# A Hedgehog attention and gMLP kernel: three-stage pipeline over batches, wide exponentials, token layout s = 4p + c

## The chip, the cores and the metric

The kernel runs on one core of a Trainium2 chip. The metric is device time in microseconds, as the median of several executions: 618.6 us before the change (runs of 616.49, 618.60 and 618.83 us).

## What is computed

Two layers run one after the other. The first is a linear attention for 8 batches, 8 heads, 576 tokens and 64 values per head:

```
phi(x):  proj = x @ w_phi                       # 64 -> 128
         proj = proj - max(|proj|)              # per token
         return [exp(proj), exp(-proj)]         # 256 features
kv  = phi(k)^T v          z = sum over tokens of phi(k)
out = (phi(q) kv) / (phi(q) z + 1e-6)
```

The heads side by side give x of 576 x 512 for each batch. The second layer, with 512 -> 1024 features, is

```
h = relu(x @ w_in);  u, v = halves of h
v_n = (v - mean(v)) / sqrt(var(v) + 1e-6)
v_s = w_spatial @ v_n + b_spatial               # over the 576 tokens
out = (u * v_s) @ w_out
```

All matmul operands are bf16 and PSUM sums are fp32. Before the change the kernel takes the exponentials of q without their row maximum; after it the maximum is subtracted. Both leave out the 1e-6 in the quotient's denominator.

## The kernel before

Work comes in 32 tasks, one for a batch and a pair of heads. A batch's 576 tokens are cut into four blocks of 128 and one of 64.

`load_batch` (L101) brings in q, k and v with 15 transfers, all issued by GpSimd, each 64 numbers (256 bytes) per token and head. `stageA` transposes q and k of two heads (L125, L131), copies them out of PSUM on ScalarE and VectorE (L128, L134) and, for each token block, makes k's projection (L139), its row maxima (L143, L147) and four exponentials of 128 columns whose bias is the row's maximum (L150, L152). q's projection is made transposed, so its features stand in partitions, in pieces of 512 and 64 tokens (L159), with two exponentials each (L162, L164). `stageB` sums k's features against v with a column of ones (L181), copies the result (L185), multiplies by q's features (L192), divides (L197, L199), transposes (L205) and copies into `xT_b` (L208).

`stage2` runs once per batch, after the batch's last pair: v's half of the first product with relu, mean, variance, a square root on ScalarE, reciprocal and normalization (L219 to L237), u's half (L247, L251), the spatial product (L259, L263), and the output product, copied out by VectorE and stored by SyncE (L269 to L275). The bias row of the spatial product stands as row 64 of the fifth token block.

The loop is software-pipelined by one task: `stageA` of task i, then `stageB` of task i-1, and `stage2` after every fourth. A scheduler puts each engine's instructions in a fixed order when the program is built. PSUM's eight banks are split into two for transposes, two shared by k's projection and the quotients, one for k's sums and three for everything else. All weights, w_spatial with its 25 transposes among them, are loaded ahead of the first batch.

## Time and profile before

| what | value |
|---|---|
| median of 3 runs | 618.6 us (616.49 to 618.83) |
| profiled execution: span from its first to its last instruction | 615.2 us |
| profiled execution: time outside the span | not recorded apart; the runs lie 1.3 to 3.6 us above the span |
| TensorE matmuls, busy | 448.6 us, 73% |
| ScalarE, busy | 380.9 us, 62% |
| VectorE, busy | 335.8 us, 55% |
| GpSimd, busy | 111.2 us, 18% |
| mean granted TensorE clock | 0.721 |

Busy time is the union of an engine's instructions. The share is an average over the whole span, so it says nothing of which engine ends which stage. The granted clock is a share of 2.4 GHz; it takes the two values 1.0 (2.4 GHz) and 0.5 (1.2 GHz), and a value between is a stretch with some of each. Matmuls overlap in the engine's pipeline, and the end of each is modelled, so a duration of one is longer than the distance from one start to the next.

### The profile page before, as it was taken

What the parts mean: (1) busy time and instruction counts of PE and PEld (TensorE: products, weight loads), DVE (VectorE), ACT (ScalarE), POOL (GpSimd) and SP (SyncE); (2) the same over time, 40 slices, a digit from 0 to 9 for tenths busy, and PEclk for the clock granted to TensorE, in tenths of its full rate; (3) what the DMA queues carried; (4) which work ended last, traced back from release to release, by engine and by line L of the source; (5) the groups of instructions that cost most, each with busy time, mean ns of one, the idle gap of its engine ahead of it and who ended that gap; (6) DMA issues with size and microseconds to landing.
All of it is one profiled execution on the core that took longest, in us unless ns stands there. A gap on an engine that the chain in (4) does not pass through costs nothing.

```text
span 615.2 us, 8892 instructions
## 1 busy us (share of the span) xinstructions
PE 448.6 (73%) x2969; PEld 219.4 (36%) x2969; DVE 335.8 (55%) x1243; ACT 380.9 (62%) x1116; POOL 111.2 (18%) x144
## 2 busy tenths in 40 slices
...
GB/s 126 125 113 18 58 58 2 18 60 78 38 2 69 21 70 34 1 78 55 62 0 1 78 77 39 1 69 22 70 35 0 78 2 1 0 29 50 1 2 77
DMA packets 119966, 26.47 MB, mean 43 GB/s; under 512 B 113712, under 2 KB 114800, under 8 KB 119920
## 3 DMA queue, kind: packets, MB, share of 16 engines
...
## 4 chain that ended last, share of the span: by engine, by line
PE 47%; ACT 36%; DVE 7%; DMA 5%; issue 3%; POOL 1%; DVEq 0%; ACTq 0%; POOLq 0%
ACT k_feat L152 8%; ACT k_feat L150 7%; PE ps_kv L181 7%; PE ps_v L219 6%; PE ps_s L259 6%; PE ps_num L192 5%; ACT q_featT L162 5%; PE ps_u L247 5%; PE ps_o L269 5%; ACT q_featT L164 4%; PE ps_k L131 4%; DMA w_sp_tmp<-in_moe_w_spatial_dram 3%; ACT qT L128 3%; PE ps_qp L159 3%; ACT L231 3%
## 5 line engine op out<-in xcount | busy, mean ns | idle before, releaser
L150 ACT ACTIVATE k_feat<-ps_kp,negm 128x128 bf16<-128x128 f32 (+1 forms) x320 | 121.9, 381 | 23.7 <-DVE negm L143 23.4
L152 ACT ACTIVATE k_feat<-ps_kp,m 128x128 bf16<-128x128 f32 (+1 forms) x320 | 122.5, 383 | 8.2 <-DVE negm L143 4.1
L143 DVE TENSOR_REDUCE negm<-ps_kp 128x2 f32<-128x256 f32 (+1 forms) x160 | 67.4, 423 | 80.9 <-PE ps_kp L139 67.4
L162 ACT ACTIVATE q_featT<-ps_qp 128x512 bf16<-128x512 f32 (+1 forms) x128 | 53.7, 424 | 91.4 <-PE ps_qp L159 91.4
L139 PE MATMUL ps_kp<-wphi,kT 128*128 128x256 bf16 (+1 forms) x160 | 57.8, 364 | 52.3 <-ACT k_feat L152 44.3
L181 PE MATMUL ps_kv<-v_aug,k_feat 128*128 128x65 bf16 (+1 forms) x640 | 81.6, 229 | 15.0 <-ACT k_feat L150 14.8
L110 POOL DMA_DIRECT2D q_bf<-in_q_dram x40 | 34.8, 873 | 278.6 <-PE ps_q L125 277.2
L181 PEld LDWEIGHTS <-k_feat 128*128 128x128 bf16 (+1 forms) x640 | 48.1, 111 | 98.0 <-ACT k_feat L150 80.8
L199 DVE TENSOR_SCALAR attn_pair<-ps_num,recip 128x64 bf16<-128x64 f32 (+1 forms) x320 | 71.4, 273 | 1.1
L247 PE MATMUL ps_u<-xT_b,w_in_bf 128*128 128x512 bf16 (+1 forms) x256 | 55.7, 371 | 18.0 <-ACT uT L251 14.3
L219 PE MATMUL ps_v<-w_in_bf,xT_b 128*128 128x512 bf16 (+1 forms) x160 | 68.0, 573 | 1.1 <-DVE xT_b L208 0.9
L128 ACT COPY qT<-ps_q 128x576 bf16<-128x576 bf16 x32 | 20.7, 646 | 76.3 <-PE ps_q L125 61.0
L192 PE MATMUL ps_num<-kv_sb,q_featT 128*128 128x65 bf16 (+1 forms) x640 | 55.2, 233 | 12.5 <-ACT k_feat L152 9.4
L197 DVE RECIPROCAL recip<-ps_num 128x2 f32<-128x2 f32 (+1 forms) x160 | 26.6, 169 | 59.3 <-PE ps_num L192 57.4
L164 ACT ACTIVATE q_featT<-ps_qp 128x512 bf16<-128x512 f32 (+1 forms) x128 | 53.4, 421 | 0.0
L192 PEld LDWEIGHTS <-q_featT 128*128 128x128 bf16 (+1 forms) x640 | 41.4, 125 | 29.0 <-issue 23.7
L247 PEld LDWEIGHTS <-w_in_bf 128*128 128x128 bf16 x256 | 23.4, 117 | 61.7 <-issue 56.7
L205 PE MATMUL ps_a<-ident,attn_pair 128*128 128x128 bf16 (+1 forms) x160 | 43.1, 270 | 1.1 <-DVE attn_pair L199 0.9
L159 PE MATMUL ps_qp<-qT,wphi_two 64*128 64x64 bf16 (+1 forms) x128 | 32.9, 384 | 15.1 <-ACT q_featT L164 13.4
L114 POOL DMA_DIRECT2D v_aug<-in_v_dram x40 | 34.1, 872 | 47.5 <-PE ps_qp L159 47.4
L259 PE MATMUL ps_s<-w_spatT,v_n 128*128 128x512 bf16 (+2 forms) x320 | 40.9, 285 | 0.0
L147 DVE TENSOR_SCALAR m<-negm 128x2 f32<-128x2 f32 (+1 forms) x160 | 33.4, 209 | 12.4 <-DVE negm L143 0.5
...
## 6 DMA issues: line engine op xcount, KB each, us to landing
...
q_bf<-in_q_dram POOLq DMA_DIRECT2D x32, 128.0 KB, 4.5
k_bf<-in_k_dram POOLq DMA_DIRECT2D x32, 128.0 KB, 4.6
v_aug<-in_v_dram POOLq DMA_DIRECT2D x32, 128.0 KB, 4.8
...
out_dram<-out_sb SPq DMA_DIRECT2D x8, 128.0 KB, 2.3
...
w_out_bf<-in_moe_w_out_dram POOLq DMA_DIRECT2D x4, 128.0 KB, 6.7
```

The costliest lines, as they stand in the source:

```text
L139: nc.tensor.matmul(out=ps_kp[:sl, :], lhsT=kT[:, s0:s0 + sl], rhs=wphi2, start=True, stop=True)
L143: nc.vector.tensor_reduce(out=negm2[:sl, :], in_=ps_kp[:sl, :].rearrange("p (h f) -> p h f", h=2), axis=AX.X, op=ALU.max, apply_absolute_v ...
L150: nc.scalar.activation(out=k_feat[:sl, ci, hh, 0:F], in_=ps_kp[:sl, hh * F:(hh + 1) * F], func=AF.Exp, bias=negm2[:sl, hh:hh + 1], scale=1.0)
L152: nc.scalar.activation(out=k_feat[:sl, ci, hh, F:2 * F], in_=ps_kp[:sl, hh * F:(hh + 1) * F], func=AF.Exp, bias=m2[:sl, hh:hh + 1], scale= ...
L162: nc.scalar.activation(out=q_featT[:, hh, 0, t0:t0 + tw], in_=ps_qp[:F, :tw], func=AF.Exp, bias=0.0, scale=1.0)
L164: nc.scalar.activation(out=q_featT[:, hh, 1, t0:t0 + tw], in_=ps_qp[:F, :tw], func=AF.Exp, bias=0.0, scale=-1.0)
L181: nc.tensor.matmul(out=ps_kv[:, hh, fc, :], lhsT=k_feat[:sl, ci, hh, fc * F:(fc + 1) * F], rhs=v_aug[:sl, ci, h, :], start=(ci == 0), stop ...
L192: nc.tensor.matmul(out=ps_num[:sl, hh, :], lhsT=q_featT[:, hh, fc, s0:s0 + sl], rhs=kv_sb[:, hh, fc, :], start=(fc == 0), stop=(fc == 1))
L199: nc.vector.tensor_scalar(out=attn_pair[:sl, ci, hh * D:(hh + 1) * D], in0=ps_num[:sl, hh, 0:D], scalar1=recip2[:sl, hh, :], scalar2=None, ...
L219: nc.tensor.matmul(out=ps_v[:sl, :], lhsT=xT_b[:, kc, s0:s0 + sl], rhs=w_in_bf[:, kc, HALF:DFF], start=(kc == 0), stop=(kc == KC - 1))
L247: nc.tensor.matmul(out=ps_u[:, :tw], lhsT=w_in_bf[:, kc, dc * P:(dc + 1) * P], rhs=xT_b[:, kc, t0:t0 + tw], start=(kc == 0), stop=(kc == K ...
L259: nc.tensor.matmul(out=ps_s[:, :tw], lhsT=v_n[:kl, sc, dc * P:(dc + 1) * P], rhs=w_spatT[:kl, sc, t0:t0 + tw], start=(sc == 0), stop=(sc = ...
```

## The change

The kernel's body is written anew around the same arithmetic.

* **Layout.** Token s = 4p + c stands in partition p, so that one transfer brings four tokens (1 KB) per partition and head, and a batch has four full blocks of 128 rows. The 64 tokens beyond 512 of two batches stand together in one tile of 128 rows (the "tail").
* **k.** The exponentials are taken over 512 columns (four blocks of a head) without a bias. The row maxima go into v instead: GpSimd multiplies v by exp(-m) for the first half of the features and by exp(m) for the second (`scale_v`). v is loaded in fp32 by SyncE.
* **q.** The row maxima are found on a second, untransposed projection, brought into bf16 high and low parts by GpSimd, transposed, and subtracted in PSUM by a third matmul against a selection matrix (`main_m`, `a2_unit`).
* **Quotient.** One reciprocal and one multiplication for four heads.
* **Second layer.** It runs for two batches at once, on nine blocks of 128 tokens. The reciprocal square root is a power of -0.5 on GpSimd, for four blocks at a time. ScalarE copies the outputs. `u` is multiplied in place.
* **Order.** Step n does the first stage of batch n, the second (q's features, k's sums) of batch n-1 and the third (quotients) of batch n-2, with the second layer of an earlier batch pair merged in between from step 4 on. The last pair's second layer stands alone at the end. The first batch's k and q are loaded ahead of the weights, and w_spatial is transposed in step 1.
* **PSUM.** One bank for all transposes, three for projections, two for sums and quotients, two for the second layer.

The core of the diff:

```diff
+    def load(b):
+        d = dict(
+            q=ld.tile([P, H, NB * D], BF16, tag="q_bf", name="q_bf"),
...
+        nc.gpsimd.dma_start(out=d["k"], in_=main_ap(k, b))
+        nc.gpsimd.dma_start(out=d["q"], in_=main_ap(q, b))
+        nc.sync.dma_start(out=d["v"].rearrange("p (h c) d -> p h (c d)", h=H), in_=main_ap(v, b))
...
+    def a1_unit(b, pj):
...
+        kT = a1.tile([P, 2, 2, P], BF16, tag="kT")
+        nc.scalar.copy(out=kT, in_=pt[:, 0])
+        nc.scalar.copy(out=d["qT"][:, pj].rearrange("p h (c t) -> p h c t", c=2), in_=pt[:, 1])
         for hh in range(2):
             h = 2 * pj + hh
+            pk = ps_pj.tile([P, NB, F], FP32, tag="pj")
+            for cp in range(2):
+                nc.tensor.matmul(out=pk[:, 2 * cp:2 * cp + 2, :], lhsT=kT[:, hh, cp, :], rhs=wphi2,
+                                 start=True, stop=True)
+            kf = feat.tile([P, 2, NB, F], BF16, tag="kf", bufs=10)
+            d["kf"][h] = kf
+            nc.vector.tensor_reduce(out=d["mk"][:, 0, h, :], in_=pk, axis=AX.X, op=ALU.max,
+                                    apply_absolute_value=True)
+            nc.scalar.activation(out=kf[:, 0], in_=pk, func=AF.Exp, bias=0.0, scale=1.0)
+            nc.scalar.activation(out=kf[:, 1], in_=pk, func=AF.Exp, bias=0.0, scale=-1.0)
...
+            nc.vector.tensor_reduce(out=d["mq"][:, h, :], in_=pq, axis=AX.X, op=ALU.max,
+                                    apply_absolute_value=True)
+    def scale_v(b, pj):
...
+        nc.scalar.activation(out=em[:, 0, :], in_=mk, func=AF.Exp, bias=0.0, scale=-1.0)
+        nc.scalar.activation(out=em[:, 1, :], in_=mk, func=AF.Exp, bias=0.0, scale=1.0)
...
+        for i in range(2):
+            nc.gpsimd.tensor_tensor(out=vs[:, i, :, 0:D], in0=d["v"][:, 2 * pj * NB:(2 * pj + 2) * NB, :],
+                                    in1=em[:, i, :].unsqueeze(2).to_broadcast([P, 2 * NB, D]), op=ALU.mult)
+        nc.gpsimd.tensor_copy(out=vs[:, :, :, D:DA].rearrange("p i n o -> p i (n o)"), in_=em)
...
+    def a2_unit(b, pj):
...
+            for par in range(2):
+                nc.tensor.matmul(out=pq[:, par, :], lhsT=wphi2[:, par * F:(par + 1) * F],
+                                 rhs=d["qT"][:, pj, hh, :], start=(par == 0), stop=False)
+            nc.tensor.matmul(out=pq.rearrange("p a t -> p (a t)"), lhsT=sel[:, h, :],
+                             rhs=mT[b % 2][:, 0:NB, :].rearrange("p c t -> p (c t)"), start=False, stop=True)
...
+            nc.scalar.activation(out=qf[:, 0, :], in_=pqf, func=AF.Exp, bias=0.0, scale=1.0)
+            nc.scalar.activation(out=qf[:, 1, :], in_=pqf, func=AF.Exp, bias=0.0, scale=-1.0)
...
+    def norm_half(pn, x, i):
+        rc = small.tile([P, 4, 1], FP32, tag="rc", bufs=4)
+        nc.vector.reciprocal(out=rc, in_=pn[:, :, D:DA])
+        nc.vector.tensor_tensor(out=x[:, 4 * i:4 * i + 4, :], in0=pn[:, :, 0:D],
+                                in1=rc.to_broadcast([P, 4, D]), op=ALU.mult)
...
-            nc.scalar.activation(out=rstd[:sl, :], in_=mv[:sl, 1:2], func=AF.Sqrt,
-                                 bias=eps_b[:sl, :], scale=1.0)
+        nc.gpsimd.tensor_tensor(out=rstd[:, 0:n], in0=var[:, 0:n], in1=neghalf[:, 0:n].unsqueeze(2), op=ALU.pow)
...
-            nc.vector.tensor_copy(out=out_sb[:sl, :], in_=ps_o[:sl, :])
+        nc.scalar.copy(out=ob, in_=po)
...
+    load(0)
+    load_tail(0)
+    raw = load_weights()
+    load(1)
+    left = []
+    for n in range(B + 2):
+        a = a_tasks(n)
+        if n == 1:
+            a.insert(0, lambda: transpose_spatial(*raw))
+        b = []
+        if n >= 4 and n % 2 == 0:
+            ts = b_tasks((n - 4) // 2)
+            b, left = ts[:len(ts) // 2], ts[len(ts) // 2:]
+        elif left:
+            b, left = left, []
+        merge(a, b)
+    merge([lambda: None], b_tasks(G - 1))
```

How the order of instructions changes is shown at three places. The first is ScalarE before the change, in the second layer of a batch: exponentials (L150, L152), relus (L224, L251), the square root (L231) and the loads of its function tables.

```order
L231 ACT_TABLE_LOAD
L231 ACTIVATE rstd<-mv,eps_b 128x1 [waits DVE_49] x2
L152 ACT_TABLE_LOAD
L152 ACTIVATE k_feat<-ps_kp,m_1216 128x128
L224 ACTIVATE v_relu<-ps_v 128x512 [waits DVE_49,PE_49,Activation_49] x2
L150 ACTIVATE k_feat<-ps_kp,negm_1225 128x128 [waits PE_49]
L152 ACTIVATE k_feat<-ps_kp,m_1226 128x128
```

After the change, ScalarE in step 5: relus of u (L431), the two copies of transposed k and q (L197, L198), k's exponentials (L209, L210), the exponentials of the maxima (L226, L227) and q's exponentials (L311, L312).

```order
L431 ACTIVATE uT<-pu 128x512 [waits PE_49]
L209 ACTIVATE kf<-pk 128x512 [waits DVE_49]
L210 ACTIVATE kf<-pk 128x512
L209 ACTIVATE kf<-pk 128x512 [waits DVE_49]
L210 ACTIVATE kf<-pk 128x512
L226 ACTIVATE em<-mk 128x8 [waits Pool_49]
L227 ACTIVATE em<-mk 128x8
L311 ACTIVATE qf<-pq 128x512 [waits PE_49]
L312 ACTIVATE qf<-pq 128x512
```

The table loads are gone, every large instruction is 512 wide, and k's exponentials wait for VectorE's maximum although they no longer read it (both read the same PSUM bank).

The second place is the start of GpSimd, before the change: the first batch's q and k stand behind all weights.

```order
L77 DMA w_in_bf<-in_moe_w_in_dram 128x1024 x4
L81 DMA w_out_bf<-in_moe_w_out_dram 128x512 [waits DMASW0_49]
...
L86 DMA w_sp_tmp<-in_moe_w_spatial_dram 128x576 [waits DMASW4_49]
L92 DMA w_spatT<-in_moe_b_spatial_dram 1x16x36 [waits DMASW5_49]
L110 DMA q_bf<-in_q_dram 128x8x64 [waits DMASW6_49]
L112 DMA k_bf<-in_k_dram 128x8x64 [waits DMASW7_49]
```

After it, GpSimd zeroes eight tiles (seven of them shown) and then issues k and q of batch 0.

```order
L86 MEMSET mT_102 128x640
L83 MEMSET mhl_104 128x640
L86 MEMSET mT_106 128x640
L89 MEMSET mhl_t 128x128
L91 MEMSET mT_t 128x128
L95 MEMSET vst_112 128x2112
L95 MEMSET vst_114 128x2112
L176 DMA k_bf<-in_k_dram 128x8x256
L177 DMA q_bf<-in_q_dram 128x8x256
...
L108 DMA w_in_bf<-in_moe_w_in_dram 128x1024 [waits DMASW0_49]
```

The zeroing has come ahead of the first load, and the weights have gone behind it.

The third place is TensorE in step 5 after the change: output products of one batch pair (L471), transposes (L194), q's projection with its selection matmul (L304, L306) and k's sums (L337) of three other batches.

```order
L471 MATMUL po<-w_out_bf,uT 128x512
L194 LDWEIGHTS k_bf [waits DVE_49]
L194 MATMUL pt<-ident,k_bf 128x128 [waits PE_49]
...
L471 LDWEIGHTS uT
L471 MATMUL po<-w_out_bf,uT 128x512
L304 LDWEIGHTS wphi_90
L304 MATMUL pq<-qT,wphi_90 128x256 [waits DVE_49]
...
L306 MATMUL pq<-mT_102,sel 128x512
L471 LDWEIGHTS uT
L471 MATMUL po<-w_out_bf,uT 128x512
...
L337 MATMUL pv<-vs,kf 128x65
```

Before the change the row has k's projection and k's sums by turns, here outside the second layer:

```order
L139 MATMUL ps_kp<-wphi_87,kT 128x256 [waits Activation_49]
L181 LDWEIGHTS k_feat [waits Activation_49]
L181 MATMUL ps_kv<-v_aug,k_feat 128x65 [waits DMASW1_49]
L139 LDWEIGHTS kT [waits DVE_49]
L139 MATMUL ps_kp<-wphi_87,kT 64x256 [waits Activation_49]
L181 LDWEIGHTS k_feat [waits Activation_49]
```

The large matmuls of the second layer now stand between the small ones of the first, instead of in a stretch of their own.

## Rows read from the trace of the kernel before

**Rows 1.** The page: span, and busy time of each engine

```profile
span 615.2 us, 8892 instructions
...
PE 448.6 (73%) x2969; PEld 219.4 (36%) x2969; DVE 335.8 (55%) x1243; ACT 380.9 (62%) x1116; POOL 111.2 (18%) x144
```

**Rows 2.** Busy time by stretch; the columns are named in the first line

```profile
core 0: us, PE busy (x) PEld busy (x) DVE busy (x) ACT busy (x) POOL busy (x), PEclk, DMA share, GB/s
...
257.00:329.00 72.00, 56.49 (x366) 27.51 (x366) 40.72 (x150) 47.73 (x140) 12.60 (x15) 0.63 0.44 42
```

**Rows 3.** The page: the chain that ended last, by engine

```profile
PE 47%; ACT 36%; DVE 7%; DMA 5%; issue 3%; POOL 1%; DVEq 0%; ACTq 0%; POOLq 0%
```

**Rows 4.** Groups by form: shapes, count, busy us, mean ns, idle before, releaser

```profile
L152 ACT ACTIVATE k_feat<-ps_kp,m 128x128 bf16<-128x128 f32 x256 | 99.3, 388 | 8.1 <-DVE negm L143 4.1 <-DVE m L147 3.1
...
L143 DVE TENSOR_REDUCE negm<-ps_kp 128x2 f32<-128x256 f32 x128 | 54.1, 424 | 55.8 <-PE ps_kp L139 42.3 <-PE ps_kv L181 12.7
...
L162 ACT ACTIVATE q_featT<-ps_qp 128x512 bf16<-128x512 f32 x64 | 38.9, 608 | 91.4 <-PE ps_qp L159 91.4
...
L231 ACT ACT_TABLE_LOAD x22 | 28.2, 1283 | 0.4
...
L263 DVE TENSOR_TENSOR gatedT<-ps_s,uT 128x512 bf16<-128x512 f32 x32 | 22.1, 692 | 19.6 <-PE ps_s L259 18.7 <-ACT k_feat L152 0.8
...
L197 DVE RECIPROCAL recip<-ps_num 128x2 f32<-128x2 f32 x128 | 21.5, 171 | 46.1 <-PE ps_num L192 44.3
...
L228 DVE BATCH_NORM_STATS2 stats<-v_relu 128x6 f32<-128x512 bf16 x32 | 20.5, 683 | 6.6 <-ACT v_relu L224 6.6
...
L162 ACT ACTIVATE q_featT<-ps_qp 128x64 bf16<-128x64 f32 x64 | 15.3, 240 | 0.0
...
L208 DVE COPY xT_b<-ps_a 128x576 bf16<-128x576 bf16 x32 | 14.5, 453 | 14.7 <-PE ps_a L205 14.6
...
L185 DVE CAST kv_sb<-ps_kv 128x260 bf16<-128x260 f32 x32 | 13.2, 413 | 0.2 <-PE ps_kv L181 0.2
L237 DVE TENSOR_SCALAR v_n<-v_relu,negmean,rstd 128x512 bf16<-128x512 bf16 x32 | 13.2, 413 | 1.1
```

**Rows 5.** Start, us and instruction on ScalarE, two exponentials in a row

```profile
45.82 0.58 ACT L162 ACTIVATE q_featT<-ps_qp 128x512 bf16<-128x512 f32 x1
46.29 0.59 ACT L164 ACTIVATE q_featT<-ps_qp 128x512 bf16<-128x512 f32 x1
```

**Rows 6.** The chain in order of time: start, us, what

```profile
263.74 3.96 PE ps_o L269 x17
...
314.03 4.83 PE ps_v L219 x11
```

**Rows 7.** Busy time and clock by 3 us, columns as in the second group

```profile
263.00:266.00 3.00, 2.94 (x15) 1.18 (x13) 2.19 (x4) 0.00 (x0) 0.00 (x0) 1.00 0.09 34
...
269.00:272.00 3.00, 1.80 (x25) 1.21 (x25) 2.29 (x11) 2.77 (x9) 0.00 (x0) 0.97 0.34 127
272.00:275.00 3.00, 2.75 (x15) 1.21 (x14) 1.38 (x7) 1.16 (x3) 0.00 (x0) 0.50 0.23 49
...
314.00:317.00 3.00, 3.00 (x9) 0.78 (x7) 1.96 (x8) 2.93 (x9) 0.00 (x0) 0.50 0.00 0
317.00:320.00 3.00, 2.25 (x7) 0.77 (x7) 0.70 (x4) 2.96 (x5) 0.00 (x0) 0.57 0.00 0
```

**Rows 8.** Start, us and instruction on GpSimd, first microseconds

```profile
0.74 0.20 POOL masks.py:197 MEMSET ident<- 128x128 bf16 x1 [0.29 <-POOLq L308]
...
2.01 0.32 POOL masks.py:199 TENSOR_SCALAR_AFFINE_SELECT ident<-ident 128x128 bf16<-128x128 bf16 x1
...
10.81 0.93 POOL L110 DMA_DIRECT2D q_bf<-in_q_dram  x1 [1.34 <-DMA w_in_bf<-in_moe_w_in_dram]
```

**Rows 9.** Start, us and instruction on TensorE, the first batch

```profile
37.02 0.77 PE L125 MATMUL ps_q<-ident,q_bf 128*128 128x128 bf16 x5
```

**Rows 10.** The page: transfers, KB each, median us from issue to landing

```profile
k_bf<-in_k_dram POOLq DMA_DIRECT2D x32, 128.0 KB, 4.6
```

More of the change, by code (lines that the diff above doesn't have):

```diff
@@ new lines, in num_tail @@
+    def num_tail(g):
+        d = gs[g]
+        x = a1.tile([P, H, D], BF16, tag="x", bufs=3)
+        for i in range(2):
+            pn = ps_kn.tile([P, 4, DA], FP32, tag="kn")
+            for y in range(4):
+                h = 4 * i + y
+                for bl in range(2):
+                    r = slice(bl * TL, (bl + 1) * TL)
+                    for s in range(2):
+                        nc.tensor.matmul(out=pn[r, y, :], lhsT=d["qf"][:, h, s, r],
+                                         rhs=st[2 * g + bl]["kv"][:, h, s, 0:DA], start=(s == 0), stop=(s == 1))
+            norm_half(pn, x, i)
+        return x
```

607 lines of the change are left out of this document (399 added, 208 removed).

## The prediction

> **What bounds the kernel now.** I read the page's busy times first. No engine is busy all the time: TensorE 73%, ScalarE 62%, VectorE 55% [rows 1]. The middle batches repeat every 72 us, and one of them shows TensorE busy 56.49 us, ScalarE 47.73 and VectorE 40.72 [rows 2]. So the busiest engine is filled to 0.785, and the rest is waiting on one another. The chain of waits says the same: 47% of it is TensorE, 36% ScalarE and only 7% VectorE [rows 3], two engines by turns. The groups show what ScalarE spends: exponentials of 128 columns at 388 ns, where one of 512 columns takes 608 [rows 4].
>
> TensorE's share hides a second thing. Eleven matmuls of 512 columns took 4.83 us at a granted clock of 0.50 (1.2 GHz), 1166 columns per us; seventeen of them took 3.96 us at 1.00 (2.4 GHz), 2198 per us [rows 6, 7]. The clock rose after a stretch in which the engine was busy 3.00 of 3.00 us and fell after one with 1.80 of 3.00 [rows 7]. The mean of that batch is 0.63 [rows 2]: most of it ran at 1.2 GHz because the small matmuls wait for ScalarE. A last piece stands at the start: the first q is transposed at 37.02 us [rows 9], behind all weights.
>
> **The change, engine by engine.** I count each engine's work by durations of before, then the steps.
>
> *ScalarE.* It now has 460 instructions of 512 columns (64 copies, 288 exponentials, 72 relus, 36 output copies) and 72 of 8 columns. Two exponentials of 512 columns start 0.47 us apart [rows 5], so 460 x 0.47 = 216 us; the 8-column ones lie under the 240 ns of 64 columns [rows 4], less the 0.11 us by which neighbours overlap [rows 5], 72 x 0.13 = 9 us. The sum is 225 us, 28 per batch; were none overlapped, 460 x 0.608 + 72 x 0.24 = 297 us. The table loads go: 22 of 1283 ns for the square root are 28.2 us [rows 4], and each has one back.
>
> *VectorE.* No row shows a maximum over 512 columns. Over 256 it took 424 ns [rows 4]; the bounds are 0.42 us and twice that, and I take 0.69, the 512-column row from PSUM [rows 4]: 144 x 0.69 = 99 us. The multiplication of 256 columns by a reciprocal I take as the 260-column copy, 72 x 0.413 = 30 (bounds 0.17 and 0.69); with it 72 reciprocals x 0.171 = 12, 32 copies of k's sums x 0.413 = 13, 36 copies to x x 0.45 = 16, 36 blocks of statistics x (0.683 + 0.171) = 31, 40 normalizations x 0.413 = 17, 36 products x 0.692 = 25, 22 smaller copies x 0.45 = 10 [rows 4]. The sum is 253 us, 32 per batch.
>
> *TensorE.* Columns per batch: 36,300 in the first layer (transposes, both projections of q, the selection matmul, sums, quotients) and 39,200 in the second, 75,500 in all; before it was 68,300. So the change adds work here: 34 us at 2198 columns per us, 65 us at 1166.
>
> *GpSimd.* Per batch ten two-input products of 512 columns, and the issue of loads. No row shows one. The nearest are 0.32 us for a select over 128 columns and 0.20 for zeroing 128 [rows 8]. The bounds are 0.32 us (a fixed price) and 2.6 (four times the columns, two inputs). I take 1.3: 13 us per batch, and 4 us for loads of 0.93 us each [rows 8]. That is under half of any step. Its queue is in order, and in each step a load of batch n+2 waits there for the last transposes of batch n, with two scalings of v queued behind it; the sums that want these come a step later, so it costs nothing. In the last pair a power of four columns stands on the path to the spatial product, but nine blocks of u (about 1 us each) lie ahead of that.
>
> The Trainium skill speaks against this placement (GPSIMD Engine Reference, section "Elementwise — side-by-side cycle accounting"): a two-input elementwise operation takes GpSimd about twice VectorE's time, 4497 ns against 2293 for 2048 columns. By an estimate from that page 512 columns would be 1.1 us, and my sum would stay as it is. No row here shows it.
>
> *Start.* GpSimd first zeroes eight tiles, about 7,000 columns. By zeroing 128 columns in 0.20 us, of which I take half as fixed, that is 6 to 11 us [rows 8]; k is issued at about 10 us. Its 512 KB are four times a transfer that lands in 4.6 us [rows 10]: 4.6 to 18 us, and I take 7, with q behind it. The first projection is at 20 us (15 to 37).
>
> *The steps.* In steps 0 to 3 nothing of the second layer fills the gaps, and ScalarE's chain sets the time. One pair of heads: two copies (0.94), a matmul of 512 columns at 1.2 GHz (0.44), a maximum (0.69), four exponentials (1.9), two small ones (0.26), 4.2 us, and 5 with the hand-overs. k's exponentials wait for the maximum; q's exponentials, the relus and the next copies are queued behind them, and TensorE waits for the bank. Step 0: 4 x 5 + 8 exponentials of the tail (3.8) = 24. From step 1 four exponentials of q per pair come on top (1.9): 28, with w_spatial's copies beside it on VectorE; step 2 has the tail again, 31; step 3, 28.
>
> Steps 4 to 7 have everything. The floors are 34 us on TensorE (at 2.4 GHz), 32 on VectorE, and 28 on ScalarE. Filled like the busiest engine before, 34 / 0.785 gives 44 us. That this runs at 2.4 GHz I take from the rows: at 1.2 the engine would need 65 us and be busy all the time, and after such a stretch the clock rose; at 44 us it is busy 0.78 of the time.
>
> Step 8 has no first stage: 58,000 columns, 26 us, put at 30. Step 9: 48,000, 22, put at 24. The last pair alone: 78,300 columns, 36 us, and 2 for the last store: 38.
>
> *Sum.* 20 + 24 + 28 + 31 + 28 + 4 x 44 + 30 + 24 + 38 = 399 us of span, against 615.2 [rows 1]. The runs lie 1.3 to 3.6 us above that span, so 402, which I put at 400 us.
>
> **Rivals.**
>
> *Near the floor* (0.17). The new order mixes four batches on TensorE, so it may fill better than before. With steps 4 to 7 at 35 and steps 8 and 9 at 26 and 22 the time is 402 - 36 - 6 = 360 us. For it: three engines have 28 to 34 us of work and only the busiest counts. Against it: three engines as even as that rarely all have something ready, and one bank serves all transposes.
>
> *The chain holds* (0.20). If the second layer does not fill the gaps but adds its own, a step is the 31 us of step 2, 18 us of second-layer columns (39,200 / 2198), and half a microsecond of waiting for each of 13.5 evictions: 56. That gives 4 x 12 more, and 12 more in steps 8 and 9: 460 us. For it: k's exponentials wait for VectorE, and the 24 us per batch that ScalarE sat idle before is of that kind. Against it: the second layer has two banks of its own.
>
> *The clock stays at 1.2 GHz* (0.05). Steps 4 to 7 at 65 us (+84), steps 8 and 9 at 50 + 41 (+37), the tail at 67 (+29): 552 us. It would take gaps on TensorE like that of 269 to 272 us throughout [rows 7]; against it speaks the full clock in the dense stretch of 263 to 266 us. The Trainium skill (TensorE: Matmul & The Clock Gate, section "A second HAM failure mode: psum-queue depth-cycling") says that waiting for PSUM banks between groups of matmuls can make the clock flip; the fall after 272 us is of that kind.
>
> *Slower than before: GpSimd's products* (0.03). They decide once ten of them and 4 us of loads exceed the step, at 4 us each. The kernel is slower than before when each step takes about 70 us, at 6.6 us per product; at 8 us the eight steps that scale v take 84 us each, and the time is some 750 us. The price would be 25 times the select's 0.32 us; columns and inputs explain 8 of these. That the change does not do what it says has no room here: the instructions are counted from the built order.
>
> **Chances and range.** The forecast, 400 us with its own range of 372 to 430, gets 0.55. I give 345 to 475 us: it takes in the floor and the chain, and leaves out the slow clock, GpSimd, and the outer ends of the others. About 0.5% (3 us) is what a measurement of this kernel can tell from no change. Faster by more has 0.965, within it 0.005, slower 0.03.
>
> **What would show it.** One table load; ScalarE's 512-column instructions 0.47 us apart; TensorE's first transposes before 20 us; steps 4 to 7 about 44 us each, with a granted clock above 0.9; a maximum of 512 columns near 0.69 us; GpSimd's products near 1.3 us. I am wrong if GpSimd's products take over 3 us, if the clock in the middle is 0.5, or if VectorE's maxima end most of ScalarE's waits.

## The result, and the profile after

The changed kernel takes 431.5 us (median of 4 runs, 431.1 to 432.9); the kernel before took 617.6 us beside it (4 runs, 616.2 to 618.8). The ratio is 0.699 (95% interval 0.697 to 0.701). The forecast was 400 us with a range of 345 to 475: faster, inside the range, and 31.5 us too low. The measured time lies 1.5 us above the narrower 372 to 430 that went with the forecast itself. Of run 1 below, two of four executions, both at 424.3 us, are over 1.5% above its fastest and count as slow, so its time is that of the other two. The rest of this text is about the 31.5 us and about what the gain of 186 us is made of.

The page of the changed kernel, to be read beside [rows 1, 3]: span and busy times, and the chain by engine.

```profile
span 430.8 us, 7853 instructions
...
PE 323.1 (75%) x3122; PEld 201.1 (47%) x3122; DVE 239.3 (56%) x534; ACT 247.1 (57%) x533; POOL 152.6 (35%) x236
...
PE 35%; ACT 23%; POOL 16%; DVE 12%; DMA 9%; issue 4%; ACTq 0%; POOLq 0%; DVEq 0%
```

TensorE does more columns than before (607,360 for 548,928, added up from the instructions of the two traces) in 125 us less of busy time. The new name in the chain is POOL, which is GpSimd: 1% before, 16% now. The same by steps (columns as in [rows 2]); a step runs from one batch's first transposes to the next batch's, the last rows from the quotients of batches 6 and 7 and the last pair's second layer:

```profile
0.00:15.50 15.50, 0.02 (x1) 0.02 (x2) 8.05 (x8) 1.28 (x1) 13.97 (x24) 1.00 1.07 216
15.50:70.80 55.30, 23.82 (x211) 17.18 (x212) 18.43 (x33) 17.39 (x42) 32.60 (x52) 0.66 0.92 123
70.80:99.10 28.30, 20.00 (x155) 13.08 (x155) 12.11 (x21) 21.11 (x48) 11.15 (x16) 0.68 0.31 41
99.10:136.50 37.40, 27.13 (x296) 19.99 (x296) 21.53 (x50) 24.25 (x56) 18.70 (x28) 0.79 0.45 70
136.50:169.30 32.80, 26.93 (x302) 17.51 (x302) 24.62 (x61) 25.89 (x57) 12.52 (x18) 0.84 0.38 73
169.30:211.30 42.00, 35.48 (x347) 22.14 (x346) 27.70 (x64) 29.16 (x65) 18.72 (x28) 0.96 0.27 47
211.30:252.40 41.10, 34.48 (x412) 22.35 (x411) 22.74 (x54) 28.28 (x62) 11.14 (x16) 0.95 0.46 107
252.40:305.20 52.80, 43.56 (x363) 26.37 (x362) 36.61 (x78) 32.88 (x71) 17.87 (x28) 0.88 0.06 21
305.20:333.40 28.20, 27.19 (x341) 17.72 (x340) 16.72 (x41) 20.53 (x44) 4.49 (x6) 1.00 0.25 86
333.40:363.30 29.90, 25.01 (x240) 14.65 (x239) 19.18 (x55) 20.23 (x44) 8.17 (x14) 1.00 0.01 1
363.30:390.00 26.70, 25.36 (x265) 14.11 (x264) 14.78 (x39) 9.60 (x18) 0.00 (x0) 1.00 0.19 69
390.00:430.80 40.80, 34.18 (x200) 15.97 (x199) 16.82 (x37) 16.49 (x28) 3.31 (x6) 0.98 0.22 72
```

Step 0 is the outlier: 55.3 us with TensorE busy 23.8, VectorE 18.4 and ScalarE 17.4, so these three mostly wait, while GpSimd is busy 32.6. Steps 4 to 7 are uneven; their mean is 41.0 us. The scheduler does not keep the second layer where it was written: of its matmul columns 5,120 stand in step 2, 10,240 in step 3, and 47,616 in step 6 against 31,744 in step 7. From 305 us on TensorE is busy 0.84 to 0.96 of each stretch, at a granted clock of 0.98 to 1.00.

TensorE at the start, beside [rows 9] (start, us, instruction, idle time before it and its releaser):

```profile
15.48 0.61 PE L194 MATMUL pt<-ident,k_bf 128*128 128x128 bf16 x4 [15.48 <-DMA k_bf<-in_k_dram]
...
25.01 0.38 PE L261 MATMUL pq<-wphi,kqT 128*128 128x256 bf16 x2 [1.38 <-ACT kf_t L256]
39.55 0.38 PE L337 MATMUL pv<-vs,kf 128*128 128x65 bf16 x4 [14.15 <-POOL vs L233]
...
45.29 0.29 PE L282 MATMUL pt<-ident,mhl_t 128*128 128x128 bf16 x1 [2.58 <-POOL mhl_t L280]
45.95 0.58 PE L194 MATMUL pt<-ident,k_bf 128*128 128x128 bf16 x4 [0.38 <-DVE mT_t L283]
```

and GpSimd in the same stretch:

```profile
18.85 0.54 POOL L112 DMA_DIRECT2D wsp<-in_moe_w_spatial_dram  x1
...
29.24 0.51 POOL L117 DMA_DIRECT2D w_spT<-in_moe_b_spatial_dram  x1 [3.64 <-DMA wsp<-in_moe_w_spatial_dram]
31.80 1.02 POOL L117 DMA_DIRECT2D w_spT<-in_moe_b_spatial_dram  x2 [2.05 <-DMA wspt<-in_moe_w_spatial_dram]
...
36.29 0.94 POOL L177 DMA_DIRECT2D q_bf<-in_q_dram  x1
37.19 2.11 POOL L231 TENSOR_TENSOR vs<-v_f,em 128x512 bf16<-128x512 f32 x2
```

TensorE's queue holds batch 0's first sums of k (L337) ahead of the second pair of heads (L194 at 45.95 us). They need v scaled, and GpSimd comes to that at 37.2 us: its queue has all weights and batch 1 in front, and their issue waits for earlier transfers to land. So the second pair is transposed at 45.95 us, 30 us after the first.

The groups by form, beside [rows 4], and two exponentials in a row, beside [rows 5]:

```profile
L231 POOL TENSOR_TENSOR vs<-v_f,em 128x512 bf16<-128x512 f32 x64 | 65.7, 1048 | 144.1 <-ACT em L226 124.5 <-ACT em L227 19.5
...
L207 DVE TENSOR_REDUCE mk<-pk 128x4 f32<-128x512 f32 x64 | 42.2, 687 | 42.0 <-PE pk L203 41.0 <-PE pn L358 0.7
...
L209 ACT ACTIVATE kf<-pk 128x512 bf16<-128x512 f32 x64 | 39.4, 615 | 19.3 <-DVE mk L207 19.3
...
L347 DVE TENSOR_TENSOR x<-pn,rc 128x256 bf16<-128x256 f32 x72 | 29.1, 419 | 1.0
...
L197 ACT COPY kT<-pt 128x512 bf16<-128x512 bf16 x32 | 19.1, 596 | 80.3 <-PE pt L194 75.5 <-PE pn L358 4.8
L417 DVE TENSOR_SCALAR vn<-vr,mv,rstd 128x512 bf16<-128x512 bf16 x32 | 16.5, 568 | 10.1 <-POOL rstd L414 10.1
...
L197 ACT ACT_TABLE_LOAD x1 | 1.3, 1283 | 0.7 <-PEq L600 0.7
```

```profile
300.02 0.60 ACT L209 ACTIVATE kf<-pk 128x512 bf16<-128x512 f32 x1
300.50 0.62 ACT L210 ACTIVATE kf<-pk 128x512 bf16<-128x512 f32 x1
```

The prices were near the forecast (0.687 us for the maximum, 0.419 for 256 columns of the quotient, 0.48 between exponentials) or under it (1.05 for a product on GpSimd, where 1.3 was taken). What was missing is a wait.

### The profile page after: what moved, and what is told of

Read it like the earlier page. It is cut to its first block, busy times and chain, and to the rows that moved or that the text cites. A ratio compares the mean times of both kernels' runs of the same rounds, so it can differ in the third digit from the quotient of the medians.

```text
span 430.8 us, 7853 instructions
## 1 busy us (share of the span) xinstructions
PE 323.1 (75%) x3122; PEld 201.1 (47%) x3122; DVE 239.3 (56%) x534; ACT 247.1 (57%) x533; POOL 152.6 (35%) x236
## 4 chain that ended last, share of the span: by engine, by line
PE 35%; ACT 23%; POOL 16%; DVE 12%; DMA 9%; issue 4%; ACTq 0%; POOLq 0%; DVEq 0%
ACT kf L209 6%; PE ps L447 5%; POOL vs L231 5%; ACT kf L210 5%; PE pu L429 5%; DMA out_dram<-ob 4%; DVE mk L207 4%; ACT qf L311 3%; ACT qf L312 3%; PE pt L194 3%; PE po L471 3%; POOL vst L276 3%; PE pk L203 3%; DMA wspt<-in_moe_w_spatial_dram 3%; PE pv L397 2%
## 5 line engine op out<-in xcount | busy, mean ns | idle before, releaser
L231 POOL TENSOR_TENSOR vs<-v_f,em 128x512 bf16<-128x512 f32 x64 | 65.7, 1048 | 144.1 <-ACT em L226 124.5
L207 DVE TENSOR_REDUCE mk<-pk 128x4 f32<-128x512 f32 x64 | 42.2, 687 | 42.0 <-PE pk L203 41.0
L197 ACT COPY kT<-pt 128x512 bf16<-128x512 bf16 x32 | 19.1, 596 | 80.3 <-PE pt L194 75.5
L209 ACT ACTIVATE kf<-pk 128x512 bf16<-128x512 f32 x64 | 39.4, 615 | 19.3 <-DVE mk L207 19.3
L218 DVE TENSOR_REDUCE mq<-pq 128x4 f32<-128x512 f32 x64 | 43.9, 685 | 9.6 <-PE pq L215 8.7
L337 PE MATMUL pv<-vs,kf 128*128 128x65 bf16 x512 | 30.5, 201 | 21.0 <-POOL vs L233 17.9
L397 PE MATMUL pv<-w_in_bf,xT 128*128 128x512 bf16 x144 | 40.9, 408 | 5.0 <-ACT vr L401 4.3
L311 ACT ACTIVATE qf<-pq 128x512 bf16<-128x512 f32 x64 | 40.2, 627 | 7.3 <-PE pq L306 7.2
L474 ACT COPY ob<-po 128x512 f32<-128x512 f32 x36 | 21.1, 598 | 35.8 <-PE po L471 25.7
L358 PE MATMUL pn<-kv,qf 128*128 128x65 bf16 x512 | 37.0, 198 | 5.0 <-ACT qf L312 2.0
L312 ACT ACTIVATE qf<-pq 128x512 bf16<-128x512 f32 x64 | 40.6, 634 | 0.0
L337 PEld LDWEIGHTS <-kf 128*128 128x128 bf16 x512 | 26.9, 103 | 28.8 <-issue 22.8
L210 ACT ACTIVATE kf<-pk 128x512 bf16<-128x512 f32 x64 | 39.7, 620 | 0.0
L471 PE MATMUL po<-w_out_bf,uT 128*128 128x512 bf16 x144 | 38.0, 386 | 0.4 <-ACT ob L474 0.2
L358 PEld LDWEIGHTS <-qf 128*128 128x128 bf16 x512 | 27.6, 100 | 18.4 <-ACT qf L311 4.6
L429 PE MATMUL pu<-xT,w_in_bf 128*128 128x512 bf16 x128 | 34.2, 402 | 2.1 <-ACT uT L431 1.3
L447 PE MATMUL ps<-w_spT,vn 128*128 128x512 bf16 x128 | 33.9, 379 | 0.0
L203 PE MATMUL pk<-wphi,kT 128*128 128x256 bf16 x128 | 25.9, 320 | 10.1 <-ACT kT L197 5.1
L341 DVE CAST kv<-pv 128x260 bf16<-128x260 f32 x32 | 13.5, 423 | 34.1 <-PE pv L339 34.0
L431 ACT ACTIVATE uT<-pu 128x512 bf16<-128x512 f32 x32 | 19.1, 614 | 20.1 <-PE pu L429 20.0
## 6 DMA issues: line engine op xcount, KB each, us to landing
wsp<-in_moe_w_spatial_dram POOLq DMA_DIRECT2D x1, 576.0 KB, 10.1
```

The lines of the kernel that those rows point to most:

```text
L207: nc.vector.tensor_reduce(out=d["mk"][:, 0, h, :], in_=pk, axis=AX.X, op=ALU.max, apply_absolute_value=True)
L209: nc.scalar.activation(out=kf[:, 0], in_=pk, func=AF.Exp, bias=0.0, scale=1.0)
L210: nc.scalar.activation(out=kf[:, 1], in_=pk, func=AF.Exp, bias=0.0, scale=-1.0)
L231: nc.gpsimd.tensor_tensor(out=vs[:, i, :, 0:D], in0=d["v"][:, 2 * pj * NB:(2 * pj + 2) * NB, :], in1=em[:, i, :].unsqueeze(2).to_broadcast ...
L311: nc.scalar.activation(out=qf[:, 0, :], in_=pqf, func=AF.Exp, bias=0.0, scale=1.0)
L312: nc.scalar.activation(out=qf[:, 1, :], in_=pqf, func=AF.Exp, bias=0.0, scale=-1.0)
```

## The experiments

All times are medians; a difference is against 431.5 us. The scheduler orders every engine anew for each edit, so an edit can also change the order elsewhere; where it did, the text says so.

**1. Weights late**

```diff
-    raw = load_weights()
     load(1)
+    raw = []
...
-        if n == 1:
+        if n == 3:
             a.insert(0, lambda: transpose_spatial(*raw))
...
+        if n == 0:
+            a.append(lambda: raw.extend(load_weights()))
```

> Edit: the loads of w_in, w_spatial, the bias and w_out are issued after the first step's work instead of before it, and the transposes of w_spatial move from step 1 to step 3. Theory (GpSimd's in-order queue): the first scaling of v, at 37.2 us in the changed kernel, starts before 26 us, because batch 1's loads and the tail loads are all that is left ahead of it; the second unit's transposes, at 46.0 us, come before 33 us, and with the moved transposes batch 1's first transposes come at 45 to 50 us instead of 70.8. Time 431.5 - 20 - 7 = 404 us (398 to 412). Rival (given back later): the second layer waits for weights that now land later, or the later steps are bound by TensorE anyway and simply start sooner and idle; then 425 us or more although the early rows move.

Measured: 418.6 us (from 417.1 and 420.1, too few for an interval), 12.9 less. The early rows moved nearly as the theory says: the first scaling began at 23.1 us, the second pair's transposes at 33.7 instead of 46.0, batch 1's at 52.5 instead of 70.8, and step 0 took 37.2 us, 18 less. But step 2 took 45.1 instead of 37.4, so 7.7 were given back, and the next run shows where. The time lies between the theory's 412 and the rival's 425.

**2. Only the transposes of w_spatial late**

```diff
-        if n == 1:
+        if n == 3:
             a.insert(0, lambda: transpose_spatial(*raw))
```

> Edit: only the transposes of w_spatial move, from step 1 to step 3; the loads stay. Theory (they run alone, with ScalarE idle 10.3 us before batch 1's first copy, through the one bank for transposes): beside other work they are hidden, 431.5 - 7 = 424 us (421 to 427). Rival (they cost their 7 us wherever they are, since one bank serves all transposes): 430 to 433 us.

Measured: 431.8 us (ratio to before 0.700, 0.698 to 0.702). No change; the rival is right. Step 0 became 8.2 us shorter and step 2 took 6.5 more (43.9): the scheduler put the transposes at its end, from 126.9 us to batch 3's first transposes at 133.8. In the changed kernel they stand between batch 0 and batch 1:

```profile
68.19 0.59 PE L141 MATMUL pt<-ident,wsp 128*64 128x128 bf16 x4 [0.55 <-DVE w_spT L136]
...
69.50 0.58 PE L141 MATMUL pt<-ident,wsp 128*64 128x128 bf16 x4 [0.54 <-DVE w_spT L143]
...
70.83 0.58 PE L194 MATMUL pt<-ident,k_bf 128*128 128x128 bf16 x4 [0.55 <-DVE w_spT L143]
```

Each group waits 0.55 us for VectorE to empty the one bank, and the next batch's transposes wait in the same line: six groups 1.3 us apart are 7.6 us here, and 6.8 us in run 2.

**3. Batch 0's scaling on VectorE**

```diff
+            eng = nc.vector if b == 0 else nc.gpsimd
-            nc.gpsimd.tensor_tensor(out=vs[:, i, :, 0:D], ...
+            eng.tensor_tensor(out=vs[:, i, :, 0:D], ...
```

(and the same for the tail's products and the split of its maxima, for the first pair)

> Edit: for batch 0 alone the products that scale v, the tail's, and the split of the tail's maxima run on VectorE instead of GpSimd; all loads stay where they were. Theory (GpSimd's queue is what holds the first sums): the first sums of k's features start before 26 us instead of 39.5 and the second unit's transposes before 33 instead of 46; time 431.5 - 15 = 416 us (410 to 422), less than in the first experiment because batch 1 is still loaded at 35 us. Rival (the transfers themselves are late: v or the weights share the DMA engines, and what is scaled is not there): first sums after 35 us, 428 us or more.

Measured: 418.9 us (0.679, 0.676 to 0.683), 12.6 less. The first sums came at 24.3 us and the second pair's transposes at 31.2, and step 0 took 43.3 us, while all loads stood where they were:

```profile
24.34 0.29 PE L339 MATMUL pv<-vs,kf 128*128 128x65 bf16 x4 [0.61 <-DVE vs L234]
...
31.23 0.59 PE L194 MATMUL pt<-ident,k_bf 128*128 128x128 bf16 x4 [0.30 <-DVE mT_t L285]
```

So the queue was the cause of these 12 us of step 0, not the transfers. A product took 0.686 us on VectorE, where GpSimd needs 1.048. Step 0 still took 19 us more than forecast; 7.8 of them are the transposes of w_spatial.

**4. k's exponentials narrow**

```diff
-            nc.scalar.activation(out=kf[:, 0], in_=pk, func=AF.Exp, bias=0.0, scale=1.0)
-            nc.scalar.activation(out=kf[:, 1], in_=pk, func=AF.Exp, bias=0.0, scale=-1.0)
+            for c in range(NB):
+                nc.scalar.activation(out=kf[:, 0, c], in_=pk[:, c], func=AF.Exp, bias=0.0, scale=1.0)
+                nc.scalar.activation(out=kf[:, 1, c], in_=pk[:, c], func=AF.Exp, bias=0.0, scale=-1.0)
```

> Edit: k's exponentials of 512 columns are cut into pieces of 128, as the kernel before had them; all else stays. ScalarE then has 512 of them 0.25 us apart instead of 128 that are 0.48 apart: +67 us of its time (247 to about 315). Theory (ScalarE's instructions stand in a chain by turns with TensorE, about half of the time): the price is 25 to 50 us, so 456 to 482. Rival (ScalarE's idle 184 us take it): under 10 us, 441 or less. Rival (ScalarE sets the time): the full 67, 498.

Measured: 435.8 us (0.707, 0.704 to 0.709), 4.3 more. ScalarE's busy time rose by 22 us, not 67: the pieces followed each other at 0.16 us, not at the 0.25 of the kernel before.

```profile
175.92 0.28 ACT L210 ACTIVATE kf<-pk 128x128 bf16<-128x128 f32 x1
176.07 0.30 ACT L211 ACTIVATE kf<-pk 128x128 bf16<-128x128 f32 x1
```

So width alone is worth little: ScalarE's idle time takes most of the 22 us, as the first rival says.

**5. Square root on ScalarE again**

```diff
-        nc.gpsimd.tensor_tensor(out=rstd[:, 0:n], in0=var[:, 0:n], in1=neghalf[:, 0:n].unsqueeze(2), op=ALU.pow)
+        nc.scalar.activation(out=var[:, 0:n], in_=var[:, 0:n], func=AF.Sqrt, bias=0.0, scale=1.0)
+        nc.vector.reciprocal(out=rstd[:, 0:n], in_=var[:, 0:n])
```

> Edit: the twelve powers on GpSimd go back to a square root on ScalarE and a reciprocal on VectorE, so ScalarE loads a table before and after each of them: 24 loads of 1.283 us, 31 us more on ScalarE. Theory (ScalarE has idle time that takes it: 22 us more of its busy time cost 4 us in the run with narrow exponentials): 434 to 440 us. Rival (a load stands between the exponentials that TensorE waits for, so each is paid in full): 458 to 464 us.

Measured: 425.4 us (0.689, 0.686 to 0.692), 6.1 less. Both expectations missed the sign. The scheduler set neighbouring roots together, so eleven table loads came on top, 14 us, and not 24. In the changed kernel VectorE's normalizations waited 10.1 us for the power on GpSimd (group L417 above); here ScalarE waited 4.6 us for the addition that is left there, and steps 4 to 7 took 160.4 us for 164.1. This part of the change cost time; how much of it is the shorter wait, how much GpSimd's 11 us less of work and how much the new order, the run does not separate.

**6. All scaling on VectorE**

```diff
-            eng = nc.vector if b == 0 else nc.gpsimd
+            eng = nc.vector
```

(against run 3; every tail's products and splits likewise, while the batches' splits stay on GpSimd)

> Edit: as the run with batch 0's scaling on VectorE (418.9 us), but for all batches: 56 more products of v at 0.684 us, twelve of the tail's and the small copies, some 53 us more on VectorE (247 to 300). Theory (past the start GpSimd is on no path, and VectorE's idle time takes the work): the same as that run, 415 to 423 us. Rival (VectorE's maxima now stand behind the products, and k's exponentials wait for them): 432 to 445. Rival (GpSimd's tail products and masks hold TensorE in steps 2, 4 and 6 as in step 0): 405 to 412.

Measured: 399.3 us (0.649, 0.645 to 0.653), 32.2 less than the changed kernel and 19.6 less than run 3, more than the boldest rival said. VectorE went from 56% to 72% busy, and the others waited for it little more than before: by the trace, TensorE 17.2 us in all for 10.8, ScalarE 23.5 for 24.9.

```profile
PE 311.7 (79%) x3122; PEld 195.5 (50%) x3122; DVE 286.1 (72%) x662; ACT 246.2 (62%) x533; POOL 66.3 (17%) x108
```

Steps 2 to 6 took 34.2, 30.0, 36.2, 41.7 and 42.9 us; in the changed kernel 37.4, 32.8, 42.0, 41.1 and 52.8. TensorE's waits for GpSimd, 40.7 us in all in the changed kernel, are nearly gone. The large ones were (us in total, times, longest):

```profile
PE pv L337 <- POOL vs L233: 17.9, 4, 14.2
...
PE pt L282 <- POOL mhl_t L280: 11.8, 4, 3.5
...
PE pt L293 <- POOL mhl L290: 9.3, 8, 1.6
```

and in this run one, 4.1 us, is left:

```profile
PE pt L295 <- POOL mhl L292: 4.1, 4, 2.2
```

**7. The transposes of w_spatial in other banks**

```diff
-            pt = ps_tr.tile([P, S], BF16, tag="tr")
+            pt = ps_s2.tile([P, S], BF16, tag="s2")
```

> Edit: the transposes of w_spatial go through the two PSUM banks of the second layer, which are empty then, instead of the one bank for transposes; all else as in the changed kernel. Theory (the one bank makes them 7.6 us long and holds batch 1's transposes behind them; moving them to step 3 did not help because the bank went with them): 431.5 - 6 = 425 us (423 to 428). Rival (the time is given back in the steps after): 430 to 433.

Measured: 420.1 us (0.683, 0.679 to 0.687), 11.4 less, more than the theory's 423 to 428. The gain is real and its reason is not the one expected: with banks of their own the transposes moved into the hole that TensorE had while it waited for GpSimd.

```profile
27.59 0.83 PE L132 MATMUL pt<-ident,wsp 128*128 128x128 bf16 x6 [2.37 <-DMA wsp<-in_moe_w_spatial_dram]
31.34 0.24 PE L134 MATMUL pt<-ident,wspt 64*128 64x64 bf16 x1 [2.93 <-DMA wspt<-in_moe_w_spatial_dram]
...
45.73 0.59 PE L194 MATMUL pt<-ident,k_bf 128*128 128x128 bf16 x4 [0.38 <-DVE mT_t L283]
```

The second pair still came at 45.7 us, but batch 1 at 62.5 instead of 70.8.

**8. Stages of a batch one after another**

```diff
-            if 1 <= n <= B:
-                ts.append(lambda j=j: a2_unit(n - 1, j))
-                ts.append(lambda j=j: kv_unit(n - 1, j))
...
+        for j in range(NP):
+            ts.append(lambda j=j: a2_unit(n, j))
+            ts.append(lambda j=j: kv_unit(n, j))
```

(the new lines stand behind `main_m(n)`, the quotients likewise; a pair's second layer beside the next pair's first layer)

> Edit: the stages of one batch are written one after another again (first stage, second stage, quotients of the same batch, then the next batch; the second layer of a pair beside the next pair's first stages); every instruction and its width stays. Theory (mixing stages of three batches is what fills TensorE and lifts its clock; width and tables are small): the step goes from 41 us towards the 56 us that the rival of a holding chain had: 500 to 550 us, with a mean clock under 0.85. Rival (the order does not matter, since the engines' queues even it out): 445 or less.

Measured: 442.1 us (0.718, 0.715 to 0.720), 10.7 more. The theory that mixing three batches fills TensorE fails: the time is the rival's, and the mean clock was 0.915. The rival's reason, that the queues even the order out, is not what the trace shows. On TensorE the batches did stand one after another; in each of the seven cases the next batch's first transposes come after the last quotients of the batch before, here batch 5's and batch 6's:

```profile
309.82 0.42 PE L358 MATMUL pn<-kv,qf 128*128 128x65 bf16 x8
...
315.82 0.38 PE L194 MATMUL pt<-ident,k_bf 128*128 128x128 bf16 x4 [0.52 <-DVE xT L387]
```

What still stood between them is the second layer of the pair before (L397 among others): from 200 to 330 us TensorE was busy 100.7 of 130 us at a clock of 0.99. So the mixing of three batches is worth the 10.7 us here; what mixing in the second layer is worth, this run does not show.

**9. Only the splits of the maxima on VectorE**

```diff
-        nc.gpsimd.tensor_copy(out=m[:, 0:NB, 0:H], in_=mq)
-        nc.gpsimd.tensor_tensor(out=m[:, 0:NB, H:2 * H], ...
+        nc.vector.tensor_copy(out=m[:, 0:NB, 0:H], in_=mq)
+        nc.vector.tensor_tensor(out=m[:, 0:NB, H:2 * H], ...
```

(and the tail's)

> Edit: only the splits of q's maxima into high and low parts (two instructions of some 0.2 us per batch and per pair's tail) go from GpSimd to VectorE; the products that scale v stay on GpSimd. In the changed kernel TensorE's transposes of these waited 21 us in all for GpSimd (11.8 for the tails', 9.3 for the batches'). Theory (the queue: short instructions stand behind long products and TensorE's in-order queue stands behind them): most of the 20 us between the run with batch 0's scaling on VectorE and the one with all of it there comes back, 412 to 421 us. Rival (the products' own 1.05 us, since k's sums wait for scaled v): 427 to 433. Rival (the new order that came with the move made that run fast, no wait of GpSimd): 427 or more too, with the waits for the splits gone.

Measured: 407.6 us (0.662, 0.659 to 0.665), 23.9 less, under the theory's 412, with all products still on GpSimd. So three quarters of run 6's gain come without moving a product. Nor is it the wait for the splits alone: TensorE's transposes of the splits still waited 14.8 us (21.1 before), now for VectorE. In the new order they and all four pairs stand ahead of the sums:

```profile
27.04 0.26 PE L282 MATMUL pt<-ident,mhl_t 128*128 128x128 bf16 x1 [1.36 <-DVE mhl_t L280]
27.67 0.59 PE L194 MATMUL pt<-ident,k_bf 128*128 128x128 bf16 x4 [0.37 <-DVE mT_t L283]
...
39.16 0.38 PE L337 MATMUL pv<-vs,kf 128*128 128x65 bf16 x4 [2.56 <-POOL vs L233]
```

The sums came as late as ever (39.2 us), but the four pairs' transposes were done by then (the fourth began at 34.8). TensorE's waits for scaled v fell too, from 17.9 to 6.8 us, with the products as long as before. So what costs is work queued behind a wait for GpSimd; how much of the 23.9 us is the wait and how much the order that came with the edit, these runs do not separate.

**10. The folding of k's maxima undone**

```diff
+            nc.vector.tensor_scalar(out=d["mk"][:, 1, h, :], in0=d["mk"][:, 0, h, :], scalar1=-1.0, ...
...
+                nc.scalar.activation(out=kf[:, 0, c], in_=pk[:, c], func=AF.Exp, bias=d["mk"][:, 1, h, c:c + 1],
...
+        nc.vector.tensor_copy(out=vs[:, :, 0:D], in_=d["v"][:, 2 * pj * NB:(2 * pj + 2) * NB, :])
```

> Edit: the folding of k's maxima into v is undone for the 512 tokens of each batch: the maxima are negated on VectorE, k's exponentials take them as bias in pieces of 128 columns, and v is only cast to bf16 on VectorE (32 of 512 columns). The tail stays folded. GpSimd loses its 64 products, ScalarE gains some 15 to 22 us. Theory (the folding brings nothing here: what it saves on ScalarE costs more on GpSimd): close to the run with all scaling on VectorE, 392 to 408 us. Rival (the exponentials that wait for the maximum and its negation hold TensorE, as k's projection waited 44.3 us for them in the kernel before): 415 to 431 or more.

Measured: 460.5 us (0.747, 0.744 to 0.749), 29.0 more than the changed kernel and 61 more than run 6, which frees GpSimd too. The theory that folding brings nothing is wrong, and the time is beyond the rival's 431. TensorE did wait more for ScalarE, 47.2 us in all for 30.9, but not because ScalarE waited for the maxima: its waits for VectorE fell from 24.9 to 20.1 us. ScalarE was busy 306.3 us instead of 247.1, since with the row's maximum as bias the pieces start 0.25 us apart again:

```profile
155.53 0.47 ACT L212 ACTIVATE kf<-pk,mk 128x128 bf16<-128x128 f32 x1
155.79 0.47 ACT L214 ACTIVATE kf<-pk,mk 128x128 bf16<-128x128 f32 x1
```

Part of the loss is not ScalarE's 59 us, however: the tail's products stayed on GpSimd behind the loads, TensorE waited 14.3 us for them, and step 0 took 62.7 us. That is 7.4 of the 29.0 against the changed kernel, and 20.0 of the 61 against run 6. How the other 22 us divide between the bias, VectorE's 17 us of added work and the new order, no run separates.

**11. Three parts undone together** (runs 4, 5 and 8 in one kernel)

> Edit: three parts of the change undone together in the changed kernel: stages written one after another, k's exponentials in pieces of 128, square root on ScalarE. Alone they cost 10.6, 4.3 and -6.1 us. Theory (they do not stand in for one another; the gain comes from what is left: whole-batch transfers, blocks of 512 columns per hand-over, pairs in the second layer): about the sum, 431.5 + 9 = 440 us (434 to 452). Rival (each covers the others' cost: with one stage at a time ScalarE stands on the path, so that narrow exponentials and table loads are paid): 431.5 + 11 + 22 + 31 = 495, over 470.

Measured: 460.3 us (0.746, 0.743 to 0.749), 28.8 more, where the three alone add up to 8.9. So they do cover for one another, by 20 us, but not as far as the rival had it: 157 us of the gain are left without staggering, wide exponentials of k and the power.

**12. What helped, together**

Scaling and splits on VectorE, k and q of batch 0 issued ahead of the zeroing, batch 1 ahead of the weights (which come after step 0's work, as in run 1), w_spatial through the other banks, written in step 3.

> Edit: all that helped together. Scaling of v and the splits of the maxima on VectorE for all batches; the first batch's k and q issued ahead of the zeroed tiles; batch 1's loads ahead of the weights, which come after the first step's work; the transposes of w_spatial through the second layer's two PSUM banks. Theory (these are separate waits, so they add): 399.3 of the run with all scaling on VectorE, less 5 for k that is issued some 7 us sooner, 8 for the bank (step 0 was 8.0 us shorter in that run) and 3 for the splits that still waited 4.1 us: 383 us (376 to 392). Rival (VectorE, 286 us busy, now sets the pace, and the time won at the start comes back as its waits): 394 to 402.

Measured: 393.7 us (6 runs, 390.7 to 396.5; 0.639, 0.636 to 0.641), 37.8 less than the changed kernel and 5.6 less than run 6. That is the rival's edge, and its reason is not borne out: VectorE was busy 72% as in run 6, and the waits for it were the same (TensorE 18.0 us for 17.2, ScalarE 24.1 for 23.5). The parts were not separate. The hole that w_spatial's transposes had filled in run 7 is gone here, the second pair came at 34.0 us where run 6 has 31.3, and the earlier issue bought little:

```profile
11.90 0.61 PE L195 MATMUL pt<-ident,k_bf 128*128 128x128 bf16 x4 [11.90 <-DMA k_bf<-in_k_dram]
17.74 0.61 PE L195 MATMUL pt<-ident,q_bf 128*128 128x128 bf16 x4 [5.23 <-DMA q_bf<-in_q_dram]
```

k was issued at 1.3 us instead of 8.7 and came 3.6 us sooner, q at 3.8 instead of 9.8 and came 0.4 us sooner (17.74 against 18.09). In the changed kernel's first 15.5 us the DMA engines' mean share was 1.07 at 216 GB/s (first row of the steps), and v of batches 0 and 1, 1 MB each, had been issued by SyncE at 0.7 and 2.7 us. So part of what an earlier issue wins is lost again among the other transfers; what another order of the loads would win, no run shows.

## Why the prediction was right, and where it was wrong

*Sum.* Forecast against measured span: start 20, 15.5; step 0: 24, 55.3; step 1: 28, 28.3; step 2: 31, 37.4; step 3: 28, 32.8; steps 4 to 7: 176, 164.1; step 8: 30, 29.9; step 9: 24, 26.7; last pair 38, 40.8. The differences, -4.5 + 31.3 + 0.3 + 6.4 + 4.8 - 11.9 - 0.1 + 2.7 + 2.8, are the 31.8 us between 399 and 430.8. The first two terms were meant from the first projection, which came at 19.4 us where I had 20; counted so, step 0 took 51.4 us for 24.

*The step that failed* is the one on GpSimd: "the sums that want these come a step later, so it costs nothing". The engine's sum was good: 1.05 us per product for 1.3 taken, and 152.6 us busy, 19 per batch, for 17. But the sums were not a step later. The scheduler set the first of them right behind the first pair of heads, with the next pair behind them on TensorE. And I looked at the loads of batch n+2 in GpSimd's queue and not at the 20 transfers of weights and bias and batch 1's two ahead of the first product, whose issue stalled until others had landed. The runs put that wait and the order around it at 12.6 us for batch 0 (run 3) and 32.2 in all (run 6). The rest of step 0 is another matter: 7.6 us are w_spatial's, and some 12 stay without a run of their own. In run 3 the second pair began 16.1 us after the first, where I had 8.8 for a pair and the tail, and the other three pairs took 19.5 us for 15. Run 6's 399.3 us is the forecast, but that is luck: its step 0 took 42.7 us for 24 and its steps 4 to 7 149.2 for 176.

*The rule named with it.* The Trainium skill (GPSIMD Engine Reference, "Elementwise — side-by-side cycle accounting") gives GpSimd about twice VectorE's time; here it is 1.048 to 0.686 us, 1.5 times. The 1.1 us estimated from that page is nearer than my 1.3. The cost came from the queue, which a price per instruction does not show.

*w_spatial.* I put its copies "beside" step 1 on VectorE at nothing. They stood alone, 7.6 us inside step 0. Moving them to a later step gained nothing (run 2); other banks, which let them fill the hole, gained 11.4 us (run 7).

*Steps 4 to 7.* The mean of 41.0 us lies between the forecast's 44 and the 35 of the rival near the floor, but the work was not the same. By the instructions of the trace these steps hold 280,700 columns, and not four times 75,500: the scheduler had moved the rest, 15,400 columns of the second layer into steps 2 and 3 among it, which together took 11.2 us more than forecast. Per us of steps 4 to 7 that is 1711 columns, and the forecast's is 1716. So the pace was right, by two misses that cancel: TensorE was busy 0.86 of the time and not 0.785, and did 1995 columns per busy us and not 2198.

*The clock.* Its mean in steps 4 to 7 was 0.94, and 0.88 in step 6, under the 0.9 that I named as a sign. That it rises after a stretch of full work is no rule that the rows bear out. In the kernel before TensorE was busy 3.00 of 3.00 us here too, and in the 3 us after it the clock still stood at 0.50:

```profile
293.00:296.00 3.00, 3.00 (x38) 2.26 (x36) 1.69 (x9) 1.02 (x5) 0.00 (x0) 0.50 1.16 76
```

In the changed kernel the lowest clocks, 0.66 and 0.68, are in steps 0 and 1, where TensorE is busy 0.43 and 0.71 of the time. Two executions with mean clocks of 0.879 and 0.926 took 432.9 and 431.4 us; where they differ, no trace shows, since only the first has one.

*The chain holds.* Its 56 us did not come, nor the slow clock's 65. Its argument misread a row: of the 24 us per batch that ScalarE was idle before, only a small part was k's exponentials waiting for VectorE, 23.4 us (L150) and 7.2 (L152) in the whole kernel, where q's waited 91.4 us for TensorE [rows 4]. And its 13.5 evictions per batch leave out VectorE's 4.5, with which a step would have been 58 us.

*Slower than before.* That rival's sum was off: with the other terms as forecast, eight steps of 84 us make 787 us and not 750, and the kernel would be slower than before from 63 us a step, not 70. Its price, 6.6 us and more per product, was far from the 1.05.

*ScalarE and VectorE.* One table load, as said. ScalarE was busy 247 us for 225 summed from starts, VectorE 239 us for 253. VectorE's maxima ended only 19.3 us of ScalarE's waits, TensorE's transposes 75.5.

*Where the 186 us came from.* The two traces show where TensorE's time went. Of the 184.4 us between the spans 125.5 are busy time. The columns per busy us rose 1.54 times, from 1224 to 1880, and the mean granted clock of the whole span 1.22 times, from 0.721 to 0.879, so the clock does not look like all of it. The other 59 are idle time: TensorE's waits for ScalarE fell from 113.8 to 30.9 us, those for DMA from 30.1 to 17.5, and 40.7 for GpSimd were new. The first transposes alone are 21.5 us earlier (37.02 to 15.48). Shown by an edit: undoing the folding of the maxima costs 29 us net (run 10), of which 7.4 lie in step 0 for another reason. What differs on ScalarE is the bias, 0.25 us between starts for 0.16, and not the width (run 4). Staggering, width of k's exponentials and the power together are worth 29 (run 11), the power alone less than nothing. These overlap and do not make the sum. Left without a run: whole-batch transfers and full blocks in place of 64-token pieces (ScalarE 533 instructions for 1116, VectorE 534 for 1243), and the second layer by pairs and merged in between. So which of the edits took away most of the waits stays open.
